# Mixing units in another order, weight blocks at other steps, one cast and one rest for a group's queries and keys, first load in one queue

## The chip, the cores and the metric

One core of a Trainium2 chip runs the whole program. The metric is the device time in microseconds (us). The kernel before takes 1590.1 us, the median of three runs.

## What is computed

```python
# q, k, v: (8, 12, 448, 64); w_ch1: (768, 3072); w_ch2: (3072, 768)
scores = q @ k.T / sqrt(64) - log(448)
attn   = 1 / (1 + exp(-scores))                  # a sigmoid, no row sums
x      = (attn @ v), heads joined                # (8, 448, 768)
mixed  = real(fft(fft(x, axis=1), axis=2))       # over tokens, then over channels
u      = x + mixed
un     = (u - mean(u)) / sqrt(var(u) + 1e-6)
out    = u + relu(un @ w_ch1) @ w_ch2
```

## The kernel before

The program has two stages. The first, some 410 us long, holds the attention, the Fourier mixing and the preparation of the weights, side by side; the second is the feed-forward network, whose 1180 us are nearly all matmuls. The change touches the first stage only.

**Steps.** The first stage is a written order. A loop counts steps `t` up to 204, two at a time; eight steps are one *group* `gg` (four heads of a batch: two sub-groups `w` of two heads, called `g = 2*gg + w`). There are 24 groups, three to each of the 8 batches. A group has four parts of two steps:

- part 0: `half_values` of the group before, `half_scores`, then the work entered for these steps, then `values` of the group before for `w = 0`
- part 1: two `scores`, the entered work, `values` for `w = 1`
- part 2: two `scores`, the entered work, and then `mix_some`, which takes mixing units worth 4.9 us by the kernel's own costs from the list
- part 3: two `scores`, the entered work

Work is entered with `at(step, ...)`: loads, casts, rests, folds, weight steps. `pin()` fixes on each engine the order in which the program was written. So an engine that waits holds up everything written behind it on that engine.

**Attention.** A load brings a group's queries and keys (tile `qk`). A *cast* copies them to a reduced format (`qh`, `kh`) on ScalarE, a *rest* forms what the copy lost (`ql`, `kl`) on VectorE. The scores (TensorE) go to two double PSUM banks `sc`, the sigmoid (ScalarE) brings them to SBUF as `a`. For the first two sub-groups the casts run on GpSimd and VectorE.

**Mixing.** A batch's mixing consists of 36 units. GpSimd first folds the attention result `xT` into `xp` (`FOLDS`). Then four `stage_d` outputs `d` of six units each (matmuls with the cosine and sine table `cd_sb` into `psd`, copied by ScalarE to `A`); four `stage_s` units `s` (one matmul from `A` into `pss`; of a pair, the first is copied by ScalarE to `Q`, the second is added to and subtracted from `Q` by VectorE, giving `sm` and `df`); and eight `add_x` units `x` (three transposes of `xT` into `psx`, to which VectorE adds `sm` or `df`, giving `u`). All of them, and the two `av` tiles of `values`, share four PSUM banks (pool `ps_m`). Batch `b` is mixed in the groups `3b+4`, `3b+5` and `3b+6`, below called its first, second and third mixing group. The last batch is mixed behind the attention, between pieces of the network's first matmuls (`mix_rest`, `fill`).

**Weights.** 48 blocks pass through five steps: a load (SyncE, tile `wr`, 4 buffers), an absolute value on ScalarE (`wt`; each block reuses the buffer of the block five before it), a maximum on VectorE, three bit operations on VectorE (0.56, 0.96 and 0.96 us), a store to `t_dram`. The list `ends` says at which step each block's bit operations stand, and the offsets beside it when the other steps do. Later, `pair` brings the stored blocks back and scales them.

Of the kernel before, what the change touches and what calls it, by code (L numbers as in the profile page):

```python
# [52 lines left out]
def spectral_attention_ffn(tc, qk, v, w1, w2, cd, cs, ident_in, out):  # L53
# [8 lines left out]
    with ExitStack() as top:  # L62
# [19 lines left out]
        if True:  # L82
# [7 lines left out]
            cd_sb = c1.tile([128, 2, 2, 3, 193], F32, name="cd_sb")  # L90
            cs_sb = c1.tile([128, 2, 2, HM], F32, name="cs_sb")

            raw, split, att, vrs, xts = {}, {}, {}, {}, {}

            def load_qk(gg, parts=1):
                b, r = divmod(gg, NG)
                t = io.tile([128, 2 * (SQ + S)], F32, tag="qk", name="qk")
                for w in range(2):
                    o = w * (SQ + S)
                    raw[2 * gg + w] = (t[:, o:o + SQ], t[:, o + SQ:o + SQ + S])  # L100
                step = 2 * (SQ + S) // parts
                for x in range(parts):
                    cols = slice(x * step, (x + 1) * step)
                    (nc.scalar if x else nc.sync).dma_start(t[:, cols], qk[b, r][:, cols])

            def load_v(gg):
                b, r = divmod(gg, NG)
                vrs[gg] = vr = io.tile([128, 896], F32, tag="vr", name="vr")
                nc.sync.dma_start(vr, v[b, r])

            def cast(g, n, e=None):
                split[g, n, 0] = t = wk.tile([128, (SQ, S)[n]], F32R, tag=("qh", "kh")[n], name=("qh", "kh")[n])
                if g > 1:
                    nc.scalar.activation(t, raw[g][n], AF.Copy)
                else:
                    (e or nc.gpsimd).tensor_scalar(
                        out=t, in0=raw[g][n], scalar1=1.0, scalar2=0.0, op0=ALU.mult, op1=ALU.add)

            def rest(g, n):
                split[g, n, 1] = t = wk.tile([128, (SQ, S)[n]], F32R, tag=("ql", "kl")[n], name=("ql", "kl")[n])  # L120
                nc.vector.tensor_tensor(
                    out=t, in0=raw[g][n], in1=split[g, n, 0].bitcast(F32), op=ALU.subtract)

            def sigmoid(ps):
                a = wk.tile([CP, 2, SQ], F32, tag="a", name="a", bufs=ABUF)
# [4 lines left out]
            def scores(gg, n):  # L130

                w, c = divmod(n, 3)
                g = 2 * gg + w
                ps = ps_sc.tile([128, 2, 512], F32, tag="sc", name="sc")
                for n, (kn, qn) in enumerate(((0, 0), (0, 1), (1, 0))):
                    for j in range(2):
                        h = slice(j * D, (j + 1) * D)
                        nc.tensor.matmul(  # L138
                            ps[:, j, :SQ], split[g, 1, kn][h, c * CP:(c + 1) * CP], split[g, 0, qn][h],
                            start=(n == 0), stop=(n == 2))  # L140
                att[g, c] = sigmoid(ps)

# [62 lines left out]
            def mix_units(b):  # L205
                xT, xp = xts[b]
                A = fx.tile([HM, 2, 2, 386], F32, tag="A", name="A")
                ps_d, sd, ut = {}, {}, {}

                def stage_d(kp, c, par, p):  # L210
                    m = HM - kp
                    if par == 0 and p == 0:
                        ps_d[c, kp] = ps_m.tile([128, 512], F32, tag="m", name="psd")
                    ps = ps_d[c, kp]
                    nc.tensor.matmul(
                        ps[:HM, par * 193:par * 193 + 193], xp[:, kp ^ c, c, par, p],
                        cd_sb[:, c, par, p], start=(p == 0), stop=(p == 2))
                    if par == 1 and p == 2:
                        act_next.append(lambda: nc.scalar.activation(
                            A[:, kp, c].rearrange("s (i r) -> s r i", r=2),  # L220
                            ps[:HM, 0:386].rearrange("s (r i) -> s r i", r=2), AF.Copy))

                def stage_s(kp, c):
                    m = HM - kp
                    ps = ps_m.tile([128, 512], F32, tag="m", name="pss")
                    nc.tensor.matmul(
                        ps[:m, :385], cs_sb[:HM, kp, c, :m], A[:, kp, c, :385], start=True, stop=True)
                    if c == 1:
                        sd["Q", kp] = Q = fx.tile([128, 385], F32, tag="Q", name="Q", bufs=2)
                        act_next.append(lambda: nc.scalar.activation(Q[:m], ps[:m, :385], AF.Copy))  # L230
                    else:
                        Q = sd["Q", kp]
                        sd[kp] = [fx.tile([128, 385], F32, tag=n, name=n) for n in ("sm", "df")]
                        for o, op in zip(sd[kp], (ALU.add, ALU.subtract)):
                            dve_next.append(lambda o=o, op=op: nc.vector.tensor_tensor(
                                out=o[:m], in0=ps[:m, :385], in1=Q[:m], op=op))

                def add_x(kp, r, hf):

                    lo, hi = (1, HM - 1) if r and not kp else (0, HM - kp)  # L240
                    s, d = sd[kp]
                    if hf == 0:
                        ut[kp, r] = fx.tile([128, DM], F32, tag="u", name="u", bufs=4)
                    u = ut[kp, r]
                    ps = ps_m.tile([128, 512], F32, tag="m", name="psx")
                    for i in range(3):
                        nc.tensor.transpose(
                            ps[:HM - kp, i * 128:(i + 1) * 128], xT[:, hf * 3 + i, r, kp:HS:2], ident)
                    y = d if hf == r else s
                    m = HM - kp  # L250
                    ysl = y[:m, 384:0:-1] if hf else y[:m, 0:384]

                    def add():
                        nc.vector.tensor_tensor(
                            out=u[:m, hf * 384:hf * 384 + 384], in0=ps[:m, :384], in1=ysl, op=ALU.add)
                        if hf:
                            base = b * S + (0, 113, 225, 336)[2 * r + kp] - lo

                            cut = lo + (hi - lo) // 16 * 16
                            for i, j in ((lo, cut), (cut, hi)):  # L260
                                if i < j:
                                    sp_next.append(lambda i=i, j=j: nc.sync.dma_start(
                                        u_dram[base + i:base + j, :], u[i:j, :]))
                    dve_next.append(add)


                def units_d(kp, c):
                    return [(0.33, lambda par=par, p=p: stage_d(kp, c, par, p)) for par in range(2) for p in range(3)]

                def units_s(kp, c):  # L270
                    return [(0.65, lambda: stage_s(kp, c))]

                def units_x(kp, r):
                    return [(ADD_US, lambda hf=hf: add_x(kp, r, hf)) for hf in range(2)]

                last = units_d(1, 0)
                res = (units_d(0, 1) + units_d(0, 0) + units_d(1, 1) + units_s(0, 1) + last[:3] + units_s(0, 0)
                       + last[3:] + units_x(0, 0) + units_s(1, 1) + units_x(0, 1) + units_s(1, 0)
                       + units_x(1, 0) + units_x(1, 1))
                return res  # L280

            wtile = {}
            worder = [(i, f) for f in range(NFC) for i in range(2)]
# [207 lines left out]
            load_qk(0, 2)  # L491
            load_v(0)
            for g in range(2):
                cast(g, 1)
                cast(g, 0, nc.gpsimd if g else nc.vector)
                rest(g, 0)
                rest(g, 1)
            load_qk(1)
            load_v(1)
            TQ = 4 * G  # L500
# [3 lines left out]
            def at(t, fn):  # L504
                extra.setdefault(t, []).append(fn)
# [6 lines left out]
            for gg in range(1, GG):  # L512
                if gg > 1:
                    at(8 * gg - 4, lambda n=gg: load_v(n))
                    at(max(8 * gg - 12, 6), lambda g=gg: load_qk(g))
                for w in range(2):
                    for n, fn in enumerate((cast, rest)):
                        at(8 * gg - 4 + 2 * n + 2 * w, lambda g=2 * gg + w, fn=fn: (fn(g, 0), fn(g, 1)))
            at(17, lambda: nc.sync.dma_start(cd_sb, cd))
            at(22, lambda: (nc.sync.dma_start(cs_sb, cs), nc.sync.dma_start(ident, ident_in)))  # L520
            ends = sorted([(t, (-10, -3, -1, 0, 3)) for t in range(19, TP, 8)]
                          + [(t, (-11, -5, -2, 0, 3)) for t in range(32, TP, 8)]
                          + [(t, (-10, -4, -2, 0, 3)) for t in (46, 54, 62, 70, 78, 86, 94, 158)])
            for n, (t, ds) in enumerate(ends[:2 * NFC]):
                for step, d in enumerate(ds):
                    at(t + d, lambda n=n, step=step: weight(n, step))
# [537 lines left out]
```

## Time and profile before

| | |
|---|---|
| median of three runs | 1590.1 us (1589.99 to 1591.21) |
| the profiled execution: time, span | 1589.42 us, 1587.6 us |
| TensorE matmul busy | 1559.5 us, 98% |
| VectorE busy | 1287.0 us, 81% |
| ScalarE busy | 657.9 us, 41% |
| GpSimd busy | 318.4 us, 20% |
| mean granted TensorE clock | 0.997 |

The time is the device's; the span reaches from the first instruction to the last, and 1.8 us lie around it. Shares are means over two unlike stages. For the first stage the busy time by group, the waits and the timeline say more than the page does.

### The profile page before, as it was taken

The numbers are of one execution on the slowest core, as the hardware profiler recorded it, in microseconds if no ns is written. First come the engines' busy times: TensorE is split into PE (matmuls) and PEld (weight loads), VectorE is DVE, ScalarE is ACT, GpSimd is POOL, SyncE is SP. The second block draws the span as 40 slices with busy tenths as digits, with TensorE's granted clock in tenths as the row PEclk, the third lists the DMA queues.
The fourth block names the chain that finished last, engine by engine and source line by source line (L and its number), as shares of the span: only waits on it lengthen the run. The fifth ranks groups of instructions, "written<-read, shape, count | busy, mean of one in ns | idle before, by whom it ended". The sixth has DMA issues, their size and how long they took to land.

```text
span 1587.6 us, 27518 instructions
## 1 busy us (share of the span) xinstructions
PE 1559.5 (98%) x11056; PEld 1064.9 (67%) x11056; DVE 1287.0 (81%) x2396; ACT 657.9 (41%) x823; POOL 318.4 (20%) x248
## 2 busy tenths in 40 slices
PE   8999999999999999999999999999999999999998
PEld 3555565555555557777777777777777777777775
DVE  4798899973798946887888888888788878887778
ACT  7876777774545434322232323222423232313221
POOL 3532444436888820000000000000000000000000
PEclk9999999999999999999999999999999999999999
DMA  6887978973788877568667766866776776576571
GB/s 244 299 295 284 347 262 291 335 246 107 249 280 295 323 304 304 186 262 277 236 199 304 231 235 235 295 204 267 259 254 181 282 298 232 166 296 255 200 270 50
DMA packets 130400, 402.43 MB, mean 253 GB/s; under 512 B 68833, under 2 KB 70113, under 8 KB 111713
## 3 DMA queue, kind: packets, MB, share of 16 engines
q1 hardware_dynamic: 130128, 400.22, 70.6%
q8 instruction: 86, 1.41, 0.4%
q10 hardware_dynamic: 144, 0.46, 0.1%
q14 instruction: 42, 0.34, 0.1%
HBM read 311.39 MB, written 73.92 MB: 243 GB/s over the span
## 4 chain that ended last, share of the span: by engine, by line
PE 66%; DVE 5%; DMA 2%; issue 1%; ACT 1%; SPq 0%; DVEq 0%; ACTq 0%
PE psf L815 29%; PE pso L871 29%; PE po L599 4%; PE psh L579 3%; DVE wp L439 1%; DMA ws<-w_dram 1%; DMA U<-u_dram 1%; DVE F L821 1%; DVE H L821 0%; ACT H L850 0%; DVE hl L587 0%; DVE ur L620 0%; DVE ur L899 0%; DVE acc L948 0%; DVE acc L886 0%
## 5 line engine op out<-in xcount | busy, mean ns | idle before, releaser
L815 PE MATMUL psf<-ut,ws 128*128 128x256 f16 x4536 | 506.7, 273 | 1.9 <-DVE ur L620 1.2
L871 PE MATMUL pso<-ws,H 128*128 128x384 f16 x3024 | 503.4, 326 | 1.0 <-DVE H L821 0.9
L815 PEld LDWEIGHTS <-ws 128*128 128x128 f16 x4536 | 443.4, 98 | 62.0 <-DMA ws<-w_dram 2.1
L871 PEld LDWEIGHTS <-H 128*128 128x128 f16 x3024 | 295.6, 98 | 189.9 <-DVE H L821 1.7
L840 ACT ACTIVATE F<-F 128x1024 f32<-128x1024 f32 x72 | 76.1, 1057 | 406.6 <-DVE F L821 406.6
L886 DVE TENSOR_TENSOR acc<-pso,acc 128x384 f32<-128x384 f32 x399 | 207.8, 550 | 19.9 <-PE pso L871 19.9
L821 DVE TENSOR_TENSOR H<-F,H 128x1024 f16<-128x1024 f32 (+1 forms) x144 | 155.3, 1087 | 48.8 <-ACT H L850 48.6
L126 ACT ACTIVATE a<-sc 128x900 f32<-128x900 f32 x168 | 147.5, 920 | 56.4 <-PE sc L138 50.7
L850 ACT ACTIVATE H<-F 128x1792 f16<-128x1792 f32 x72 | 122.2, 1697 | 111.0 <-DVE F L821 111.0
L821 DVE TENSOR_TENSOR F<-X,psf 128x256 f32<-128x256 f32 x288 | 117.1, 418 | 59.1 <-PE psf L815 55.1
L447 POOL TENSOR_TENSOR wq<-wq 128x384 f32<-128x384 f32 x96 | 150.5, 1573 | 32.5 <-DVE wp L439 26.9
L821 DVE TENSOR_TENSOR F<-F 128x256 f32<-128x256 f32 x288 | 109.5, 421 | 24.8 <-ACT F L840 20.1
L176 PE MATMUL av<-a,vr 128*64 128x450 f32 x576 | 119.1, 549 | 0.0
L439 DVE SCALAR_TENSOR_TENSOR wp<-wq,wsc,wp 128x1536 f16<-128x1536 f32 x48 | 99.4, 2104 | 21.8 <-ACT wp L437 21.8
L821 DVE TENSOR_TENSOR X<-X,psf 128x256 f32<-128x256 f32 x216 | 89.8, 416 | 18.6 <-PE psf L815 16.9
L579 PE MATMUL psh<-ut,wp 128*128 128x512 f16 x432 | 98.5, 379 | 0.0
L196 POOL TENSOR_TENSOR eo<-xT 128x450 f32<-128x450 f32 x48 | 53.4, 1132 | 205.1 <-ACT xT L184 198.1
L829 ACT ACTIVATE X<-psf 128x256 f32<-128x256 f32 x72 | 27.8, 386 | 155.5 <-PE psf L815 155.5
L599 PE MATMUL po<-wp,hh 128*128 128x256 f16 (+1 forms) x384 | 88.5, 326 | 0.0
L437 ACT ACTIVATE wp<-wq,wsc 128x1536 f16<-128x1536 f32 x48 | 73.5, 1570 | 25.0 <-DMA wq<-t_dram 20.7
L176 PEld LDWEIGHTS av<-a,vr 128*64 128x64 f32 x576 | 37.1, 136 | 69.6 <-issue 69.6
L579 PEld LDWEIGHTS <-wp 128*128 128x128 f16 x432 | 42.2, 98 | 49.1 <-issue 0.5
(87 smaller groups left out, 1623.6 us busy)
## 6 DMA issues: line engine op xcount, KB each, us to landing
ws<-w_dram SPq DMA_DIRECT2D x144, 1344.0 KB, 8.8
wr<-w_in SPq DMA_DIRECT2D x48, 768.0 KB, 7.8
w_dram<-wp SPq DMA_DIRECT2D x24, 1344.0 KB, 8.8
qk<-qk_in SPq DMA_DIRECT2D x23, 898.0 KB, 8.5
t_dram<-wt SPq DMA_DIRECT2D x48, 384.0 KB, 6.1
wq<-t_dram SPq DMA_DIRECT2D x24, 768.0 KB, 6.6
vr<-v_in SPq DMA_DIRECT2D x24, 448.0 KB, 5.1
U<-u_dram SPq DMA_DIRECT2D x24, 384.0 KB, 5.4
```

The costliest lines, as they stand in the source:

```text
L126: nc.scalar.activation(a, ps[:, :, :SQ], AF.Sigmoid, bias=-math.log(S), scale=1.0 / math.sqrt(D))
L176: nc.tensor.matmul(ps[j * D:(j + 1) * D, :SQ], vr[:, h:h + D], a[:, j], start=False, stop=(c == 2))
L439: nc.vector.scalar_tensor_tensor(out=w[:, 1, part], in0=t, scalar=sc, in1=w[:, 0, part], op0=ALU.mult, op1=ALU.subtract)
L447: nc.gpsimd.tensor_tensor(out=t[:, o], in0=t[:, x], in1=t[:, y], op=op)
L579: nc.tensor.matmul(hs[c, f], l[:, m], r[:, m], start=(m == n == 0), stop=(m == NCC - 1 and n == 2))
L599: nc.tensor.matmul(po[n][:, at:at + hi - lo], l[:, cols], r[:, lo:hi], start=(f == 0 and m == 0 and at == 0), stop=(f == NFC - 1 and m == ...
L815: nc.tensor.matmul(ps[:, :TH], w[:, x, a, m * 128:(m + 1) * 128], ut[y][:, b, m], start=(m == n == 0), stop=(m == n == 2))
L821: nc.vector.tensor_tensor(out=o, in0=x, in1=y, op=op)
L840: nc.scalar.activation(F[:, 0:4], F[:, 0:4], AF.Relu)
L850: nc.scalar.activation(hts[P][:, 0], F[:, 1:8], AF.Copy)
L871: nc.tensor.matmul(ps[:, :384], H[:, x, a, tp * 128:(tp + 1) * 128], w[:, y, b], start=(j == n == 0 and half != 1), stop=(j == 1 and n == ...
L886: later(0, lambda: nc.vector.tensor_tensor(out=to, in0=ps[:, :384], in1=to, op=ALU.add))
```

## The change

It has four parts.

1. The units of a batch's mixing stand in another order. With `d0 d1 d2 d3`, `s0` to `s3` and `x0` to `x7` in the order of their lists, they were `d0 d1 d2 s0 d3(1-3) s1 d3(4-6) x0 x1 s2 x2 x3 s3 x4 x5 x6 x7`. Now they are `d0 d1 s0 d2(1-2) s1 d2(3-5) x0 d2(6) x1 d3(1) x2 d3(2-6) s2 x3 s3 x4 x5 x6 x7`.
2. The weight blocks start at step 11 instead of 19 (and 24 instead of 32), and the extra ones, by which some groups hold three blocks instead of two, stand at steps 34, 58, 82, 154, 162, 178 instead of 46, 54, 62, 70, 78, 86, 94, 158. So the extra blocks of the first three batches fall into a first mixing group each.
3. Queries and keys of a sub-group are cast by one ScalarE instruction of 898 columns instead of two of 450 and 448, and their rest is one VectorE instruction. For the first two sub-groups ScalarE casts the keys and VectorE the queries; GpSimd casts nothing.
4. The two halves of the first load are both issued by SyncE; before, ScalarE issued the second.

```diff
-            def cast(g, n, e=None):
-                split[g, n, 0] = t = wk.tile([128, (SQ, S)[n]], F32R, tag=("qh", "kh")[n], name=("qh", "kh")[n])
+            def cast(g):
+                hi, lo = (wk.tile([128, SQ + S], F32R, tag=n, name=n) for n in ("hi", "lo"))
+                split[g] = [[x[:, :SQ] for x in (hi, lo)], [x[:, SQ:] for x in (hi, lo)], hi, lo]
                 if g > 1:
-                    nc.scalar.activation(t, raw[g][n], AF.Copy)
...
+                    nc.scalar.activation(hi, raws[g], AF.Copy)
+                    return
+                nc.scalar.activation(split[g][1][0], raw[g][1], AF.Copy)
+                nc.vector.tensor_scalar(
+                    out=split[g][0][0], in0=raw[g][0], scalar1=1.0, scalar2=0.0, op0=ALU.mult, op1=ALU.add)
+
+            def rest(g, n=slice(0, SQ + S)):
+                hi, lo = (x[:, n] for x in split[g][2:])
+                nc.vector.tensor_tensor(out=lo, in0=raws[g][:, n], in1=hi.bitcast(F32), op=ALU.subtract)
...
-                    (nc.scalar if x else nc.sync).dma_start(t[:, cols], qk[b, r][:, cols])
+                    nc.sync.dma_start(t[:, cols], qk[b, r][:, cols])
...
-                res = (units_d(0, 1) + units_d(0, 0) + units_d(1, 1) + units_s(0, 1) + last[:3] + units_s(0, 0)
...
+                return (d[0] + d[1] + s[0] + d[2][:2] + s[1] + d[2][2:5] + x[:1] + d[2][5:] + x[1:2] + d[3][:1]
+                        + x[2:3] + d[3][1:] + s[2] + x[3:4] + s[3] + x[4:])
...
-            ends = sorted([(t, (-10, -3, -1, 0, 3)) for t in range(19, TP, 8)]
...
+            ends = sorted([(t, (-10, -3, -1, 0, 3)) for t in range(11, TP, 8)]
+                          + [(t, (-11, -5, -2, 0, 3)) for t in range(24, TP, 8)]
+                          + [(t, (-10, -4, -2, 0, 3)) for t in (34, 58, 82, 154, 162, 178)])
```

What this moves is seen at three places. On TensorE, in the second mixing group of batch 0 (`psd` are the `d` units, `pss` the `s`, `psx` the `x`), before:

```order
L215 MATMUL psd<-cd_sb,xp 113x193 x3
L226 MATMUL pss<-A,cs_sb 113x385
L215 MATMUL psd<-cd_sb,xp 113x193 x3
L226 MATMUL pss<-A,cs_sb 113x385
L215 MATMUL psd<-cd_sb,xp 113x193 x3
L247 MATMUL psx<-ident,xT 113x128 x6
```

and in the changed kernel:

```order
L217 MATMUL psd<-cd_sb,xp 113x193
L228 MATMUL pss<-A,cs_sb 113x385
L217 MATMUL psd<-cd_sb,xp 113x193 x3
L249 MATMUL psx<-ident,xT 113x128 x3
L217 MATMUL psd<-cd_sb,xp 113x193
L249 MATMUL psx<-ident,xT 113x128 x3
L217 MATMUL psd<-cd_sb,xp 113x193
L249 MATMUL psx<-ident,xT 113x128 x3
L217 MATMUL psd<-cd_sb,xp 113x193 x3
```

The second `s` of the pair stands one unit behind the group's start instead of seven, and `x` and `d` units follow it; the seventh row, the first unit of `d3`, takes the bank that the second `s` held, and so stands behind `sm` and `df` on VectorE.

On TensorE, in the third mixing group, before:

```order
L226 MATMUL pss<-A,cs_sb 112x385
L247 MATMUL psx<-ident,xT 113x128 x6
L226 MATMUL pss<-A,cs_sb 112x385
L247 MATMUL psx<-ident,xT 112x128 x12
L138 MATMUL sc<-qh,kh 128x450 x2
```

and now:

```order
L217 MATMUL psd<-cd_sb,xp 113x193 x2
L228 MATMUL pss<-A,cs_sb 112x385
L249 MATMUL psx<-ident,xT 113x128 x3
L228 MATMUL pss<-A,cs_sb 112x385
L249 MATMUL psx<-ident,xT 112x128 x12
```

The last two units of `d3` have moved into this group, one `x` has left it, and the second `s` reads the `A` that ScalarE copies from the `d3` finished here.

On VectorE, in the second mixing group of batch 6, where `wp` is a scaled weight pair, before:

```order
L439 SCALAR_TENSOR_TENSOR wp_3840<-wq,wsc,wp_3840 128x1536
L235 TENSOR_TENSOR sm<-pss,Q 113x385
L235 TENSOR_TENSOR df<-pss,Q 113x385
L254 TENSOR_TENSOR u<-psx,df 113x384
L254 TENSOR_TENSOR u<-psx,sm 113x384
```

and now:

```order
L441 SCALAR_TENSOR_TENSOR wp_3654<-wq,wsc,wp_3654 128x1536
L237 TENSOR_TENSOR sm<-pss,Q 113x385
L237 TENSOR_TENSOR df<-pss,Q 113x385
L256 TENSOR_TENSOR u<-psx,df 113x384
L256 TENSOR_TENSOR u<-psx,sm 113x384 x2
```

The scaling of the weight pair stands ahead of `sm` as before, and a third addition `u` has come into the group.

More of the change, by code (lines that the diff above doesn't have):

```diff
@@ L91, in spectral_attention_ffn @@
             cs_sb = c1.tile([128, 2, 2, HM], F32, name="cs_sb")
-            raw, split, att, vrs, xts = {}, {}, {}, {}, {}
+            raw, raws, split, att, vrs, xts = {}, {}, {}, {}, {}, {}
             def load_qk(gg, parts=1):
@@ L100, in load_qk @@
                     raw[2 * gg + w] = (t[:, o:o + SQ], t[:, o + SQ:o + SQ + S])
+                    raws[2 * gg + w] = t[:, o:o + SQ + S]
                 step = 2 * (SQ + S) // parts
@@ L109, in load_v @@
                 nc.sync.dma_start(vr, v[b, r])
-            def cast(g, n, e=None):
-                split[g, n, 0] = t = wk.tile([128, (SQ, S)[n]], F32R, tag=("qh", "kh")[n], name=("qh", "kh")[n])
+            def cast(g):
+                hi, lo = (wk.tile([128, SQ + S], F32R, tag=n, name=n) for n in ("hi", "lo"))
+                split[g] = [[x[:, :SQ] for x in (hi, lo)], [x[:, SQ:] for x in (hi, lo)], hi, lo]
                 if g > 1:
[L114 to L122, printed above, removed]
+                    nc.scalar.activation(hi, raws[g], AF.Copy)
[6 more added lines that the diff above has]
+                nc.vector.tensor_tensor(out=lo, in0=raws[g][:, n], in1=hi.bitcast(F32), op=ALU.subtract)
             def sigmoid(ps):
@@ L138, in scores @@
                         nc.tensor.matmul(
-                            ps[:, j, :SQ], split[g, 1, kn][h, c * CP:(c + 1) * CP], split[g, 0, qn][h],
+                            ps[:, j, :SQ], split[g][1][kn][h, c * CP:(c + 1) * CP], split[g][0][qn][h],
                             start=(n == 0), stop=(n == 2))
@@ L274, in units_x @@
                     return [(ADD_US, lambda hf=hf: add_x(kp, r, hf)) for hf in range(2)]
-                last = units_d(1, 0)
-                res = (units_d(0, 1) + units_d(0, 0) + units_d(1, 1) + units_s(0, 1) + last[:3] + units_s(0, 0)
-                       + last[3:] + units_x(0, 0) + units_s(1, 1) + units_x(0, 1) + units_s(1, 0)
-                       + units_x(1, 0) + units_x(1, 1))
-                return res
+                d = [units_d(kp, c) for kp in range(2) for c in (1, 0)]
+                x = [u for kp in range(2) for r in range(2) for u in units_x(kp, r)]
+                s = [units_s(kp, c) for kp in range(2) for c in (1, 0)]
+                return (d[0] + d[1] + s[0] + d[2][:2] + s[1] + d[2][2:5] + x[:1] + d[2][5:] + x[1:2] + d[3][:1]
+                        + x[2:3] + d[3][1:] + s[2] + x[3:4] + s[3] + x[4:])
             wtile = {}
@@ L493, in spectral_attention_ffn @@
             for g in range(2):
[L494 to L497, printed above, removed]
+                cast(g)
+                rest(g, slice(0, SQ))
+                rest(g, slice(SQ, SQ + S))
             load_qk(1)
@@ L517, in spectral_attention_ffn @@
                     for n, fn in enumerate((cast, rest)):
-                        at(8 * gg - 4 + 2 * n + 2 * w, lambda g=2 * gg + w, fn=fn: (fn(g, 0), fn(g, 1)))
+                        at(8 * gg - 4 + 2 * n + 2 * w, lambda g=2 * gg + w, fn=fn: fn(g))
             at(17, lambda: nc.sync.dma_start(cd_sb, cd))
             at(22, lambda: (nc.sync.dma_start(cs_sb, cs), nc.sync.dma_start(ident, ident_in)))
-            ends = sorted([(t, (-10, -3, -1, 0, 3)) for t in range(19, TP, 8)]
-                          + [(t, (-11, -5, -2, 0, 3)) for t in range(32, TP, 8)]
-                          + [(t, (-10, -4, -2, 0, 3)) for t in (46, 54, 62, 70, 78, 86, 94, 158)])
+            ends = sorted([(t, (-10, -3, -1, 0, 3)) for t in range(11, TP, 8)]
+                          + [(t, (-11, -5, -2, 0, 3)) for t in range(24, TP, 8)]
+                          + [(t, (-10, -4, -2, 0, 3)) for t in (34, 58, 82, 154, 162, 178)])
             for n, (t, ds) in enumerate(ends[:2 * NFC]):
```

## The prediction

> **What bounds the kernel now.** I read the busy time by stage first. TensorE is busy nearly everywhere, so a gain must come from where it stands still or runs slowly; a view of the waits over the mixing groups says why it stands, and the busy time by group says where. In the rows below, one group each, the columns are the stretch in us, its length, and for each engine the busy time (and instructions), then TensorE's granted clock, the share of DMA and GB/s.
>
> ```profile
> 65.42:81.33 15.91, 15.91 (x108) 9.60 (x104) 11.25 (x19) 12.63 (x20) 6.03 (x7) 1.00 0.70 258
> 81.33:99.41 18.08, 16.63 (x103) 9.01 (x99) 16.65 (x29) 12.00 (x18) 5.93 (x6) 0.91 0.80 290
> 115.32:132.88 17.56, 16.45 (x109) 9.57 (x105) 13.03 (x21) 12.51 (x20) 6.92 (x7) 1.00 0.94 350
> 132.88:152.98 20.10, 18.08 (x102) 9.29 (x98) 18.75 (x32) 12.71 (x20) 5.95 (x7) 0.84 0.72 264
> 168.98:185.34 16.36, 16.18 (x108) 9.60 (x104) 12.41 (x21) 12.49 (x20) 5.90 (x6) 1.00 0.97 357
> 185.34:202.70 17.36, 14.91 (x102) 8.01 (x98) 17.01 (x27) 11.02 (x17) 7.70 (x7) 1.00 0.87 302
> 234.46:250.67 16.21, 14.88 (x102) 8.03 (x98) 15.93 (x25) 11.62 (x18) 7.94 (x7) 1.00 0.88 281
> 282.43:298.68 16.25, 14.89 (x102) 8.03 (x98) 15.97 (x25) 11.60 (x18) 8.03 (x7) 1.00 0.97 273
> 330.50:345.53 15.03, 14.57 (x103) 8.12 (x98) 12.34 (x22) 11.13 (x17) 6.08 (x6) 1.00 0.77 254
> ```
>
> These are the second and third mixing groups of batch 0, of batch 1 and of batch 2, then the third of 3, 4 and 5. A second group without a wait takes 15.91 us (first row); a third one needs 14.57 (TensorE's busy time in the last row) and takes up to 20.10. Two things are to be seen: where the third groups are long VectorE is full (16.65, 18.75, 17.01 us), and in two the clock was granted at 0.91 and 0.84. Over these groups VectorE is what TensorE waits for, and five times ScalarE stands behind a weight store:
>
> ```profile
> PE psx L247 <- DVE u L254: 6.3, 5, 2.4
> ACT wt L303 <- DMA t_dram<-wt: 10.7, 5, 3.2
> ```
>
> The clock falls behind such waits. In batch 0's third group three short ones (timeline of TensorE, the bracket is the wait and its releaser) precede two microseconds at half the clock (busy time by stretch again):
>
> ```profile
> 92.68 1.05 PE L247 MATMUL psx<-ident,xT 128*112 128x128 f32 x6 [0.55 <-DVE u L254]
> 94.16 0.59 PE L247 MATMUL psx<-ident,xT 128*112 128x128 f32 x3 [0.43 <-ACT Q L230]
> 95.22 0.90 PE L247 MATMUL psx<-ident,xT 128*112 128x128 f32 x3 [0.47 <-DVE df L235]
> ```
>
> ```profile
> 96.00:98.00 2.00, 2.00 (x11) 1.77 (x12) 2.00 (x5) 0.35 (x1) 1.34 (x2) 0.50 1.02 426
> ```
>
> **Weight blocks.** The same 48 blocks take the same loads, copies, bit operations and stores; only their steps move. Before, batches 0 to 2 had three blocks in each group, VectorE 3.4 us more each than with two. Now the third block lies in first mixing groups, where mixing asks nothing of VectorE. A `wt` buffer came free, by the list, 5 steps ahead of its next use at six blocks, and the five waits of 10.7 us are such places; now it is 8 or more until step 155, then once 5 (step 160) and once 6. The stores and loads stand earlier in SyncE's queue by as much as their blocks; the first load, now at step 1, goes ahead of the load for group 2, which isn't needed for 12 steps. So the old waits of batches 0 to 2 should go: third groups 18.08 + 20.10 + 17.36 - 3 x 14.57 = 11.83, second groups 17.56 + 16.36 - 2 x 15.91 = 2.10, together 13.9 us.
>
> **The new order, third mixing group.** It brings a wait of its own. The second `s` reads the `A` of the `d3` finished two units before, which ScalarE copies behind two sigmoids and the cast. What stands there in batch 3:
>
> ```profile
> 242.57 1.73 ACT L126 ACTIVATE a<-sc 128x900 f32<-128x900 f32 x2 [0.32 <-PE sc L138]
> ...
> 243.01 0.90 PE L226 MATMUL pss<-A,cs_sb 113*112 113x385 f32 x2
> ...
> 243.75 0.82 PE L247 MATMUL psx<-ident,xT 128*113 128x128 f32 x6
> ...
> 244.18 0.58 ACT L114 ACTIVATE qh<-qk 128x450 fp32r<-128x450 f32 x1
> ...
> 244.40 0.81 PE L226 MATMUL pss<-A,cs_sb 113*112 113x385 f32 x2
> ...
> 244.65 0.58 ACT L114 ACTIVATE kh<-qk 128x448 fp32r<-128x448 f32 x1
> ...
> 245.12 0.49 ACT L230 ACTIVATE Q<-pss 112x385 f32<-112x385 f32 x1
> ...
> 246.52 0.37 PE L247 MATMUL psx<-ident,xT 128*112 128x128 f32 x1 [1.31 <-DVE u L254]
> ```
>
> Mixing starts at 243.01, ScalarE is free of the casts at 245.12, 2.11 later. An `x` takes 0.33 (two between 243.75 and 244.40), an `s` 0.65, a `d` 0.33 (rows of batch 3 below). TensorE is done with two `d`, `s` and `x` at 0.66 + 0.65 + 0.33 = 1.64; `A` is there at 2.02 + 0.53 = 2.55 (0.09 for the shorter cast), so `s` waits 0.9. The last `x` takes its bank, behind `sm` and `df`: `s` ends at 3.25, 0.2 until VectorE starts and 1.0 for both give 4.45, TensorE is there at 4.2: 0.25 more. I take 1.2 us in each of six batches. Batches 0 to 2: 3.6 instead of 13.9, -10.3. Batches 3 to 5 lose 16.21 + 16.25 + 15.03 - 3 x 14.57 = 3.8 today: 3.6 instead, -0.2. The `d` units that the third group gains and the `x` it loses (0.3) the second gives back.
>
> **The new order, second mixing group.** The first unit of `d3` is there at 0.36 + 0.65 + 0.99 + 0.33 x 3 = 3.0 us after mixing starts, and waits for `df`. Before, nothing of TensorE waited for VectorE here. In batches 0 to 2 VectorE is free in time. In batches 3 and 4 it carries the normalization, and is late:
>
> ```profile
> 208.72 0.96 DVE L317 SCALAR_TENSOR_TENSOR wt<-wr,wt 128x768 int32<-128x768 int32 x1
> ...
> 227.13 1.24 PE L215 MATMUL psd<-cd_sb,xp 128*113 128x193 f32 x6
> 227.28 1.34 DVE L312 TENSOR_SCALAR wt<-wt 128x768 int32<-128x768 int32 x1
> ...
> 228.21 0.81 PE L226 MATMUL pss<-A,cs_sb 113*113 113x385 f32 x2
> ...
> 228.86 1.15 PE L215 MATMUL psd<-cd_sb,xp 128*113 128x193 f32 x6
> ...
> 229.85 0.81 PE L226 MATMUL pss<-A,cs_sb 113*113 113x385 f32 x2
> ...
> 230.31 1.62 DVE L317 SCALAR_TENSOR_TENSOR wt<-wr,wt 128x768 int32<-128x768 int32 x1
> ...
> 231.85 0.55 DVE L235 TENSOR_TENSOR sm<-pss,Q 113x385 f32<-113x385 f32 x1
> ...
> 232.32 0.55 DVE L235 TENSOR_TENSOR df<-pss,Q 113x385 f32<-113x385 f32 x1
> ```
>
> `df` is done at 232.87, 5.74 after the start of mixing at 227.13: a wait of 2.75 as it stands. But the three bit operations run beside GpSimd's folds and take 1.34 + 1.62 + 1.62, where the second and third take 0.96 without it (first row) and the first 0.56. Four joined rests ahead of them, each 0.07 us shorter by my estimate (0.62 us for 450 columns and 0.95 for 768 leave 0.15 for an instruction's start, about half of it hidden by the one before), and what they spare beside an earlier fold put VectorE about a microsecond ahead, and then most of the first operation runs before the fold starts: I take 1.8 us, which leaves a wait of 1.0, and 0.2 for the addition that the next `x` waits for. Bounds: 0 and 2.9; taken 1.2, twice: +2.4. Batch 5 has one third block more than today, 3.4 us of VectorE in two groups; VectorE's idle time there takes it up, since the normalization is over by then (12.34 busy of 15.03 in its third group); 0, at worst 1.
>
> Batch 6 has the scaling of a weight pair ahead of `sm`:
>
> ```profile
> 370.02 1.24 PE L215 MATMUL psd<-cd_sb,xp 128*113 128x193 f32 x6
> ...
> 372.80 2.05 DVE L439 SCALAR_TENSOR_TENSOR wp<-wq,wsc,wp 128x1536 f16<-128x1536 f32 x1 [7.36 <-ACT wp L437]
> ...
> 374.77 0.55 DVE L235 TENSOR_TENSOR sm<-pss,Q 113x385 f32<-113x385 f32 x1
> ...
> 375.24 0.55 DVE L235 TENSOR_TENSOR df<-pss,Q 113x385 f32<-113x385 f32 x1
> ```
>
> `df` at 375.79 is 5.77 behind the start: TensorE waits 2.8, and hands over 2.5 later than today. A wait of that length should bring the slow clock. What that costs is read from batch 1's third group: 18.08 busy at a mean clock of 0.84, against 14.57: 3.5; batch 0's is 16.63 - 14.57 = 2.1. I take 1.7, which is half of a slow stretch of 3.4 us. Behind it TensorE waits for GpSimd today, which finishes its folds at its own time:
>
> ```profile
> 391.39 0.42 PE L215 MATMUL psd<-cd_sb,xp 128*113 128x193 f32 x1 [1.40 <-POOL xp L202]
> ```
>
> That 1.4 (and 0.2 elsewhere) is given back: 2.5 + 1.7 - 1.6 = +2.6.
>
> The Trainium skill, TensorE: Matmul & The Clock Gate, Part 1, counts activity in windows of about 3.4 us and warns of idle gaps longer than that. By this rule no wait here, the longest 2.9, would slow the clock, and batch 6 would cost 0.9 instead of 2.6. The rows of batch 0 disagree: 1.45 us of waits in three pieces slowed it. I go by the rows.
>
> **Joined casts and rests, the first load.** A cast of 898 columns by two of 0.58, whose starts lie 0.47 apart, saves about 0.09 of ScalarE, which counts only in the four groups without mixing: two casts in each make 0.7, of which I take -0.2, as little of it is waited for. On VectorE nothing waits for rests beyond what stands above. At the start ScalarE copies keys before its first sigmoid and so loads two tables instead of one:
>
> ```profile
> 1.14 1.28 ACT L126 ACT_TABLE_LOAD   x1 [1.14 <-PEq L1051]
> ...
> 5.25 0.40 DVE L116 TENSOR_SCALAR qh<-qk 128x450 fp32r<-128x450 f32 x1 [5.25 <-DMA qk<-qk_in]
> ...
> 7.12 0.92 ACT L126 ACTIVATE a<-sc 128x900 f32<-128x900 f32 x1 [4.70 <-PE sc L151]
> ```
>
> Two key copies from 5.25 (0.47 and 0.58) and a table of 1.28 end at 7.6, where the first sigmoid starts at 7.12 today. The second half of the load is issued some 0.4 us later, but the first then has the engines alone. Between 0 and 0.9: +0.4. The last batch, between the network's first matmuls, has the same new dependences with more work between them: between 0 and 1.5, +0.4.
>
> **The sum.** -10.3 - 0.2 + 2.4 + 2.6 - 0.2 + 0.4 + 0.4 = -4.9 us: the profiled execution's 1589.42 to 1584.5, and from the median of 1590.1, 0.7 above it, to 1585.2, 0.3% less. A measurement of this kernel tells 0.2%, 3.2 us, from no change.
>
> **Rivals.**
>
> *VectorE doesn't get ahead in batches 3 and 4.* If it keeps its place against TensorE, both wait 2.9 instead of 1.2, and such a wait brings the slow clock there too: 2 x (1.7 + 1.7) = 6.8, 1592.0, no difference. For it: VectorE is busy without a gap there, so 1.8 us must come from GpSimd's overlap alone. Chance 0.27.
>
> *The new wait of the third groups slows the clock.* It is 1.2 us in six groups; 1.45 sufficed in batch 0, while one wait of 2.4 in batch 2 (17.36 us at clock 1.00) did not, so where the waits fall decides. At 1.7 each, six give 10.2: 1595.4, slower; five of them suffice for slower. Against it: 1.31 in batch 3 and as much in batch 4 went without. Chance 0.16.
>
> *All the waits on VectorE vanish.* If it is a little further ahead, batches 3 and 4 lose nothing, and if batch 6's wait keeps the clock, 2.4 + 1.7 more is gained: 1581.1. Chance 0.2.
>
> My forecast has 0.37. Faster by over 0.2% (below 1586.9) are the last rival and four fifths of the forecast: 0.5. Within 0.2%: the first rival and the rest of the forecast, 0.34. Slower: 0.16. The range reaches from the last rival, less 1.1 for a start and a tail without loss, to just under the slow one: 1580.0 to 1594.5; beyond it lie most of the second rival's chance and little below. The forecast's own range is 1583 to 1588.
>
> **What the profile will show.** Right: third groups of batches 0 to 2 between 15.5 and 16.2 us at clock 1.00; no wait of ScalarE for a store before 300 us; in each third group a wait of some 0.9 of `pss` for `A`; in batch 6's second group one of 2.8 of `psd` for `df`, and the wait for GpSimd near 391 us gone. Waits of `psd` for `df` above 2 us in batches 3 and 4 would speak for the first rival, a clock under 1.00 in third groups for the second. Wrong altogether would be third groups of batches 0 to 2 as long as before: then the third block wasn't their cause.

## The result, and the profile after

The changed kernel is slower by 0.6%: 1598.88 us median (six runs, 1596.52 to 1602.63) against 1590.03 (1587.89 to 1591.21), ratio 1.0061, interval [1.0043, 1.0079]. The forecast was 1585.2, 0.3% faster. The six runs lie in two sets of three, 1596.5 to 1596.9 and 1600.9 to 1602.6. The profiled execution is the slowest of them, 1602.63 us (span 1600.8), against 1589.42 (1587.6) before.

What TensorE waits for in the first 420 us (engine, line, what is waited for: us in total, times, longest):

```profile
PE psd L217 <- DVE df L237: 9.6, 4, 3.1
PE pss L228 <- ACT A L221: 5.7, 8, 1.3
...
PE psx L249 <- DVE df L237: 3.7, 8, 2.3
```

The first two are new, the third was 1.3 us before. Busy time by group, columns as in the prediction: second and third groups of batches 0, 1 and 2, then of 3, 4 and 5:

```profile
65.28:83.25 17.97, 16.09 (x109) 9.47 (x105) 16.87 (x22) 10.95 (x15) 8.74 (x7) 1.00 0.88 319
83.25:99.26 16.01, 15.10 (x104) 8.43 (x99) 11.12 (x17) 11.22 (x16) 6.29 (x6) 1.00 0.75 272
...
115.17:130.76 15.59, 15.59 (x109) 9.45 (x105) 12.31 (x19) 10.96 (x15) 7.89 (x7) 1.00 0.76 272
130.76:146.76 16.00, 15.10 (x104) 8.42 (x99) 11.14 (x17) 11.23 (x16) 6.29 (x6) 1.00 0.83 304
...
162.68:178.26 15.58, 15.58 (x109) 9.45 (x105) 12.30 (x19) 10.97 (x15) 7.87 (x7) 1.00 0.75 265
178.26:194.27 16.01, 15.11 (x103) 8.41 (x99) 11.14 (x17) 11.23 (x16) 6.27 (x6) 1.00 0.87 309
...
210.18:230.20 20.02, 17.60 (x109) 10.40 (x105) 17.52 (x23) 11.86 (x16) 8.10 (x6) 0.91 0.72 233
230.20:246.22 16.02, 15.11 (x104) 8.43 (x100) 12.65 (x18) 11.65 (x17) 6.65 (x6) 1.00 0.66 214
...
262.12:282.28 20.16, 17.69 (x109) 10.74 (x105) 17.43 (x23) 11.56 (x16) 8.13 (x6) 0.92 0.73 239
282.28:298.28 16.00, 15.11 (x104) 8.43 (x100) 12.65 (x18) 11.81 (x17) 6.88 (x6) 1.00 0.82 260
...
314.19:335.95 21.76, 18.68 (x110) 11.54 (x105) 17.31 (x24) 12.04 (x16) 8.52 (x7) 0.84 0.89 328
335.95:351.94 15.99, 15.10 (x103) 8.44 (x99) 11.13 (x17) 11.08 (x16) 6.05 (x6) 1.00 0.64 221
```

The third groups of batches 0 to 2, 18.08, 20.10 and 17.36 us before, all take 16.0 now: that part of the forecast came. Most of the loss is in the second groups of batches 3, 4 and 5: 20.02, 20.16 and 21.76 us, where before they took:

```profile
218.59:234.46 15.87, 15.87 (x108) 9.61 (x104) 15.64 (x22) 12.56 (x20) 7.86 (x6) 1.00 0.65 191
...
266.56:282.43 15.87, 15.87 (x108) 9.61 (x104) 15.60 (x22) 12.55 (x20) 7.85 (x6) 1.00 0.85 233
...
314.59:330.50 15.91, 15.91 (x108) 9.60 (x104) 12.95 (x21) 11.91 (x19) 6.64 (x6) 1.00 0.83 295
```

(The rest is lost in batch 0's second group, 17.97 us, and from batch 6's second group on.) In batch 3 VectorE works without a gap up to `df`, and the timeline shows how TensorE comes to stand behind it:

```profile
218.67 1.34 DVE L314 TENSOR_SCALAR wt<-wt 128x768 int32<-128x768 int32 x1
218.76 0.58 PE L217 MATMUL psd<-cd_sb,xp 128*113 128x193 f32 x2
...
220.05 1.62 DVE L317 SCALAR_TENSOR_TENSOR wt<-wr,wt 128x768 int32<-128x768 int32 x1
...
221.70 1.62 DVE L319 SCALAR_TENSOR_TENSOR wt<-wr,wt 128x768 int32<-128x768 int32 x1
...
223.24 0.55 DVE L237 TENSOR_TENSOR sm<-pss,Q 113x385 f32<-113x385 f32 x1
...
223.71 0.54 DVE L237 TENSOR_TENSOR df<-pss,Q 113x385 f32<-113x385 f32 x1
...
224.31 0.58 PE L217 MATMUL psd<-cd_sb,xp 128*113 128x193 f32 x2 [2.35 <-DVE df L237]
```

Mixing starts at 218.76 and reaches the first unit of `d3` 3.20 us later; `df` ends at 224.25, 5.49 after the start, and TensorE stands 2.35 us. Behind such waits the clock halves (busy time in four stretches; the clock is the third number from the right):

```profile
226.00:229.41 3.41, 3.41 (x18) 2.22 (x16) 2.14 (x4) 0.92 (x1) 0.32 (x1) 0.50 0.95 308
277.19:280.60 3.41, 3.41 (x15) 2.82 (x16) 2.60 (x5) 0.00 (x0) 1.11 (x2) 0.50 0.97 295
328.39:335.22 6.83, 6.18 (x27) 4.76 (x31) 4.04 (x8) 0.92 (x1) 1.60 (x2) 0.50 0.92 342
383.01:386.42 3.41, 3.41 (x15) 2.83 (x16) 1.26 (x3) 0.00 (x0) 3.41 (x4) 0.50 0.34 104
```

Together 17.1 us at half speed, up to 8.5 us lost.

### The profile page after: what moved, and what is told of

Read it like the earlier page. It is cut to its first block, busy times and chain, and to the rows that moved or that the text cites. A ratio compares the mean times of both kernels' runs of the same rounds, so it can differ in the third digit from the quotient of the medians.

```text
span 1600.8 us, 27412 instructions
## 1 busy us (share of the span) xinstructions
PE 1564.5 (98%) x11056; PEld 1068.4 (67%) x11056; DVE 1282.2 (80%) x2351; ACT 656.2 (41%) x780; POOL 324.8 (20%) x245
## 4 chain that ended last, share of the span: by engine, by line
PE 66%; DVE 4%; DMA 1%; ACT 1%; issue 1%; POOL 1%; SPq 0%; DVEq 0%; ACTq 0%; POOLq 0%
PE psf L816 29%; PE pso L872 29%; PE po L600 4%; PE psh L580 3%; DVE wp L441 1%; DVE F L822 1%; DMA U<-u_dram 1%; DMA ws<-w_dram 1%; POOL wq L449 1%; DVE H L822 0%; ACT H L851 0%; DVE ur L621 0%; DVE ur L900 0%; DVE acc L949 0%; DVE acc L887 0%
## 5 line engine op out<-in xcount | busy, mean ns | idle before, releaser
L124 DVE TENSOR_TENSOR lo<-qk,hi 128x898 fp32r<-128x898 f32 (+2 forms) x50 | 57.3, 1149 | 41.2 <-ACT hi L116 41.1
L217 PE MATMUL psd<-cd_sb,xp 128*113 128x193 f32 x384 | 79.8, 344 | 9.9 <-DVE df L237 9.6
```

Source lines behind the costliest of these rows:

```text
L217: nc.tensor.matmul(ps[:HM, par * 193:par * 193 + 193], xp[:, kp ^ c, c, par, p], cd_sb[:, c, par, p], start=(p == 0), stop=(p == 2))
```

## Experiments

The theory: the new order of units costs all that is lost and more, because the first unit of `d3` in the second mixing group stands behind `df`; the weight steps alone would have been a gain. The rivals: weight blocks at late steps; the start; the joined casts and rests. Five kernels split the change into its parts (each ratio is taken against runs of the kernel before on the same chip; their medians lay between 1589.1 and 1590.0):

| kernel | order | weight steps | casts, start | median us | ratio to before, interval |
|---|---|---|---|---|---|
| before | old | old | old | 1590.03 | 1 |
| e4_casts_start_only | old | old | new | 1587.96 | 0.9997 [0.9988, 1.0006] |
| e3_steps_only | old | new | old | 1577.91 | 0.9927 [0.9914, 0.9939] |
| e1_old_order | old | new | new | 1577.75 | 0.9924 [0.9912, 0.9937] |
| e2_order_only | new | old | old | 1601.56 | 1.0081 [1.0067, 1.0095] |
| e9_order_steps | new | new | old | 1600.06 | 1.0065 [1.0052, 1.0078] |
| changed kernel | new | new | new | 1598.88 | 1.0061 [1.0043, 1.0079] |

**The old order in the changed kernel.**

```diff
-                return (d[0] + d[1] + s[0] + d[2][:2] + s[1] + d[2][2:5] + x[:1] + d[2][5:] + x[1:2] + d[3][:1]
-                        + x[2:3] + d[3][1:] + s[2] + x[3:4] + s[3] + x[4:])
+                last = units_d(1, 0)
+                res = (units_d(0, 1) + units_d(0, 0) + units_d(1, 1) + units_s(0, 1) + last[:3] + units_s(0, 0)
...
```

> The changed kernel with its mixing units in the old order; weight steps, joined casts and start stay. Theory 1 (the new order behind sm and df costs all that is lost, some 15 to 20 us from batch 3 on, and the weight steps give the 8 to 14 that batches 0 to 2 gained): 1577 to 1582 us, no wait of psd for df, clock 1.00 in batches 3 to 6. Theory 2 (the weight blocks at steps 154, 162 and 178 make VectorE late in batches 5 and 6 whatever the order): 1585 to 1590, with waits of psx for df or u and a low clock left in batches 5 and 6. Theory 3 (start and joined casts cost several us): as theory 1, but group 1 starts over 1 us later than in the kernel before and the time is 1582 to 1585.

1577.75 us: the theory's number, 21 below the changed kernel. The second groups of batches 3 and 5 (busy time by group):

```profile
205.19:221.10 15.91, 15.91 (x109) 9.60 (x104) 15.32 (x20) 12.37 (x18) 7.87 (x6) 1.00 0.66 208
...
300.87:316.78 15.91, 15.91 (x109) 9.60 (x104) 14.87 (x21) 12.44 (x18) 8.48 (x7) 1.00 0.92 335
```

In batch 3 VectorE is about as busy as in the kernel before (15.32 of 15.91 us), and TensorE waits for nothing in these groups. The late weight blocks are there too, and cost batch 5 nothing in this order.

**The new order alone, the weight steps alone, casts and start alone.** In the kernel before, each by the lines that the diff above shows.

> The kernel before with nothing but the new order of units. Theory 1: the four waits of psd for df in the second mixing groups of batches 3 to 6 (2.3 to 3.1 us each in the changed kernel) and the slow clock behind them (1.7 to 3.4 each) are here too, so 1600 to 1606 us. Theory 2: batch 5 has no block at 162 here, so its second group has no wait over 1 us, and the time is 1592 to 1597. If order and weight steps only go wrong together: 1588 to 1591.

1601.56 us, as the theory says, though not by the places it named: only batches 4 and 6 have the wait for `df`. Here the third groups of batches 0 to 2 keep their third weight block and are as long as before or longer, as in batch 2:

```profile
184.66:205.42 20.76, 17.41 (x104) 10.07 (x99) 20.21 (x29) 11.72 (x18) 10.58 (x8) 0.84 0.90 331
```

Behind such a group VectorE has caught up with TensorE: in batch 3's second group, which starts at 221.33, `df` ends 11.4 us behind the start (14.1 in the changed kernel), and the group takes 15.86 us. Two of the three bit operations ahead of it start before GpSimd's fold does (229.22), and take 0.55 and 0.96 us instead of 1.34 and 1.62:

```profile
228.61 0.55 DVE L312 TENSOR_SCALAR wt<-wt 128x768 int32<-128x768 int32 x1
229.20 0.96 DVE L315 SCALAR_TENSOR_TENSOR wt<-wr,wt 128x768 int32<-128x768 int32 x1
230.20 1.62 DVE L317 SCALAR_TENSOR_TENSOR wt<-wr,wt 128x768 int32<-128x768 int32 x1
...
232.21 0.54 DVE L235 TENSOR_TENSOR df<-pss,Q 113x385 f32<-113x385 f32 x1
```

Where the weight steps take the delay of the third groups away, it comes back in the second ones: they are worth 11.5 us in the old order and 1.5, less than the runs can tell, in the new one (1601.56 - 1600.06).

> The kernel before with nothing but the new weight steps. Theory 1: third mixing groups of batches 0 to 2 fall from 18.1, 20.1 and 17.4 us to 14.6 to 16, no wait of ScalarE for a weight store in batches 0 to 2, 1576 to 1581 us. Theory 2: the same there, but batches 5 and 6 give back 5 or more: 1582 to 1590. If the third block was not the cause of the long groups: 1589 to 1592.

1577.91 us, third groups of batches 0 to 2 at 15.0 us: the third block was their cause. Batch 5 gives nothing back; from batch 6's second group to the end 2.1 us more go by than before, with a longer wait for GpSimd's fold.

> The kernel before with the joined casts and rests and the new start, old order, old weight steps. By the prediction's terms (start +0.4, casts -0.2): 1589.5 to 1591. Theory 3 (the start costs 1.2 us, group 0 lasts 10.3 instead of 9.1): 1591 to 1592.5. Theory 4 (the rest waits for the whole joined cast, VectorE falls later behind GpSimd's folds, and third groups grow): above 1593.

No difference that can be told (0.9997). Group 1 starts at 14.49 us, in the kernel before at 14.36. These rivals fall.

> The kernel before with the new order of units and the new weight steps, casts, rests and start as before. Theory 1 (order and weight steps make the whole difference): as the changed kernel, 1596 to 1602 us, waits of psd for df in batches 0 and 3 to 5. Theory 4 (the rest that waits for a joined cast puts VectorE later, so the joined form shares in the loss): 1588 to 1594 us, with shorter waits for df.

Without the joined casts and rests the waits for `df` are no shorter (2.54, 2.59 and 3.21 us in batches 3 to 5), and the time is the same within the intervals.

**Another place for `d3`.** In the changed kernel:

```diff
-                return (d[0] + d[1] + s[0] + d[2][:2] + s[1] + d[2][2:5] + x[:1] + d[2][5:] + x[1:2] + d[3][:1]
-                        + x[2:3] + d[3][1:] + s[2] + x[3:4] + s[3] + x[4:])
+                return d[0] + d[1] + s[0] + d[2] + s[1] + x[:2] + d[3] + x[2:3] + s[2] + x[3:4] + s[3] + x[4:]
```

> The changed kernel with another order of units: d2 is finished ahead of the second s, so that the first unit of d3 takes the bank of d2 (freed by ScalarE's copy) and not that of the second s (freed by sm and df on VectorE). Theory 1a (the place of d3 in that bank is what loses the time): no wait of psd for df, second groups of batches 0 and 3 to 5 take 15.6 to 16 us at clock 1.00, the 0.7 us waits of pss for A stay, 1580 to 1585 us. Rival 1b (VectorE is late in any such order, and the next to take a bank behind df waits as long): a wait of 2 to 3 us at psx or av in the same groups, 1592 to 1600.

1581.96 us, 0.9954 [0.9941, 0.9966]. No `psd` waits for VectorE, and the second groups of batches 3 and 5 are:

```profile
207.70:223.31 15.61, 15.61 (x109) 9.50 (x105) 15.38 (x20) 11.49 (x16) 7.57 (x6) 1.00 0.67 203
...
304.59:320.24 15.65, 15.65 (x106) 9.48 (x101) 14.62 (x20) 11.58 (x16) 8.37 (x7) 1.00 0.92 341
```

So it isn't the new order as such: it is the first unit of `d3` in the bank that `df` frees, with six units between it and the `s` that `df` reads. Here it stands closer, with two units between, in a bank that ScalarE frees, and doesn't wait. Most of what is left above the old order (4 us) is in the third groups, which take 16.0 us in batches 0 to 2 and 16.7 to 16.9 in batches 3 to 5; in batches 3 and 4 a `pss` waits 1.6 us for `u`, which was not expected.

**Why `df` is late.** Two kernels take VectorE's work ahead of `df` away: one moves a block's bit operations behind the mixing, the other leaves one of them out.

```diff
-            ends = sorted([(t, (-10, -3, -1, 0, 3)) for t in range(11, TP, 8)]
+            ends = sorted([(t, (-10, -3, -1, 3, 6)) for t in range(11, TP, 8)]
```

> The changed kernel with the three bit operations (and the store) of one of the two weight blocks of each group three steps later, behind the mixing instead of ahead of sm and df on VectorE. Theory 1c (these operations, slowed beside GpSimd's folds, are what makes df late): the waits of psd for df in batches 0, 3, 4 and 5 are gone or under 0.5 us, batch 6's stays (a scaled weight pair stands there), 1582 to 1588 us. Rival (VectorE has 97% of its time taken in batches 3 and 4, so what is moved behind sm and df makes something else late): waits of psx for u or of psd for xp of 1 to 2 us each, 1590 to 1597.

1592.6 us, 1.0021 [1.0012, 1.003]: the rival's time, but not the waits that it named. Batches 0 and 5 have no wait for `df` left (batch 0's first group waits 1.39 us for `A` instead), batches 3 and 4 still wait 2.29 us; the second groups of batches 3 and 5:

```profile
209.18:229.20 20.02, 17.67 (x109) 10.67 (x105) 19.51 (x28) 11.79 (x16) 8.04 (x6) 0.91 0.65 194
...
313.04:328.85 15.81, 15.81 (x109) 9.40 (x105) 15.28 (x22) 11.44 (x16) 8.50 (x8) 1.00 1.01 389
```

In batch 3 the operations that left the second group's front were replaced by those which the first group pushed out. VectorE is busy 15.3 of 15.9 us in the first group too, so a shift gives `df` nothing there. Less work should; this kernel leaves a part of the computation out, to see what it costs:

```diff
-                    nc.vector.scalar_tensor_tensor(
-                        out=ti, in0=hi, scalar=-0x40000000, in1=ti, op0=ALU.bitwise_and, op1=ALU.bitwise_or)
+                    if ends[n][0] not in (104, 107, 112, 115, 128, 131, 136, 139):
+                        nc.vector.scalar_tensor_tensor(
+                            out=ti, in0=hi, scalar=-0x40000000, in1=ti, op0=ALU.bitwise_and, op1=ALU.bitwise_or)
```

> The changed kernel without the last of the three bit operations (the one that puts the sign back) in the eight weight blocks of the first and second mixing groups of batches 3 and 4; this part of the computation is left out. Theory 1d (VectorE has no idle time between the first group and df there, so df comes earlier by as much as is taken off ahead of it, 4 to 5 us with the folds' slowing): both waits of 2.4 us and the slow clock behind them go, the two second groups fall from 20.1 to 15.6 to 16 us, batch 5 stays, 1589 to 1592 us. Rival (df waits for Q or the matmuls ahead of it, not for VectorE's volume): 1597 to 1601.

1590.12 us, 8.8 below the changed kernel, as the theory says: the waits of batches 3 and 4 are gone. Batch 3's second group, and batch 5's, whose work is untouched:

```profile
208.51:224.11 15.60, 15.60 (x110) 9.45 (x106) 12.32 (x18) 11.62 (x16) 5.93 (x6) 1.00 0.78 208
...
303.46:324.10 20.64, 17.57 (x109) 10.60 (x105) 17.33 (x24) 11.67 (x16) 8.53 (x7) 0.92 0.91 335
```

**Batch 5's block.**

```diff
-                          + [(t, (-10, -4, -2, 0, 3)) for t in (34, 58, 82, 154, 162, 178)])
+                          + [(t, (-10, -4, -2, 0, 3)) for t in (16, 34, 58, 82, 154, 178)])
```

> The changed kernel with the extra weight block of step 162 (second group of batch 5) at step 16 instead. Theory 2, cut to this place: batch 5's second group falls from 21.8 us at clock 0.84 to 15.6 to 17, all else stays, 1591 to 1594 us. If the block there is not the cause: 1596 to 1600 and the group stays over 20 us.

1595.35 us, 1.0041 [1.0028, 1.0054]. Batch 5's second group falls to 15.60 us: the third block was its cause. The time is 1.4 above what was expected. In the profiled execution, the slowest of five, group 1 took 12.43 us (11.62 in the changed kernel) and batch 0's second group 19.78 (17.97), with a wait of 1.97 for `df` and a stretch of half clock behind it.

**The clock.** TensorE is kept busy where it would wait:

```diff
-                    for i in range(3):
+                    for i in [0, 1, 2] * (7 if 3 <= b <= 6 and (kp, r, hf) == (0, 0, 1) else 1):
```

> The changed kernel in which TensorE repeats the transposes of the second x seven times in batches 3 to 6 (18 more matmuls of 128 columns, some 2 us, just ahead of the unit that waits for df; the result is the same). Clock theory (some 8.5 of the 20 us lost are the half clock behind the waits): with TensorE busy the clock stays at 1.00 in batches 3 to 6, 1588 to 1593 us. If the clock falls for another reason than idle TensorE: 1597 to 1601. If the added matmuls only lengthen the groups: above 1601.

1593.64 us, 1.0029 [1.0018, 1.0039]: with more matmuls, 5.2 us less (0.6 above the expected range). Second groups of batches 3 and 5, and the added matmuls with the wait behind them in batch 3:

```profile
208.55:227.07 18.52, 18.05 (x128) 11.43 (x124) 17.52 (x23) 11.61 (x16) 8.12 (x6) 1.00 0.73 218
...
309.42:328.69 19.27, 18.09 (x128) 11.47 (x123) 17.31 (x24) 11.67 (x16) 8.51 (x7) 1.00 0.93 339
```

```profile
219.82 2.46 PE L249 MATMUL psx<-ident,xT 128*113 128x128 f32 x21
222.68 0.58 PE L217 MATMUL psd<-cd_sb,xp 128*113 128x193 f32 x2 [0.40 <-DVE df L237]
```

`d3` starts no earlier after the group's start, but the clock stays at 1.00, and the groups are 1.5 and 2.5 us shorter. Against the changed kernel's profiled execution the profiled one here gains 9.0; the median gains less, since other executions lose less to the clock. The granted clock over the whole execution bears this out: 0.998 to 1.000 in the eight runs of this kernel, 0.993 to 0.996 in the six of the changed one.

**Batch 6.**

```diff
-                for step, e in enumerate((0, 8 + p, 9 + p)):
+                for step, e in enumerate((0, 10, 11)):
```

> The changed kernel with the two scaled weight pairs two steps later, the first behind the last mixing units of batch 6's second group and no longer ahead of sm. By the prediction's term for batch 6 (a wait of 2.3 to 2.8, 1.7 of clock, 1.6 given back): the wait of psx for df near 383 us goes and 2.5 to 4.5 us come back, 1593 to 1596.5. If the pair is only late elsewhere (the network's first matmuls wait for it): 1597 to 1602, with a wait of psh for wp.

1594.08 us, 1.0026 [1.0016, 1.0035]; the wait near 383 us is gone, as expected. This run shows something else. Its second groups of batches 3 and 4, and in each the wait:

```profile
208.94:227.47 18.53, 16.09 (x110) 9.46 (x105) 17.53 (x23) 11.57 (x16) 8.12 (x6) 1.00 0.73 218
...
259.35:279.17 19.82, 17.45 (x110) 10.73 (x105) 17.41 (x23) 11.57 (x16) 8.12 (x6) 0.91 0.83 243
```

```profile
223.08 0.58 PE L217 MATMUL psd<-cd_sb,xp 128*113 128x193 f32 x2 [2.37 <-DVE df L237]
...
273.50 0.99 PE L217 MATMUL psd<-cd_sb,xp 128*113 128x193 f32 x2 [2.37 <-DVE df L237]
```

The same wait of 2.37 us kept the clock once and halved it once.

**A version faster than both.** The changed kernel with the old order and two blocks moved:

```diff
-                          + [(t, (-11, -5, -2, 0, 3)) for t in range(24, TP, 8)]
-                          + [(t, (-10, -4, -2, 0, 3)) for t in (34, 58, 82, 154, 162, 178)])
+                          + [(t, (-11, -5, -2, 0, 3)) for t in range(24, TP, 8) if t not in (120, 144)]
+                          + [(t, (-10, -4, -2, 0, 3)) for t in (34, 58, 70, 82, 94, 154, 162, 178)])
```

> A version meant to be faster than both: the changed kernel with the old order, and the weight blocks of steps 120 and 144 (third groups of batches 3 and 4, where TensorE still waits 1.06 us for u) at steps 70 and 94, behind the mixing of the second groups of batches 1 and 2. If VectorE's load there is all that is left of the waits: 1574.5 to 1577 us, third groups of batches 3 and 4 at 14.95 instead of 16.0 us. If the blocks at 70 and 94 crowd the buffers as the third blocks did in the kernel before: 1578 to 1582, with waits in batches 1 and 2.

1574.3 us, 0.9907 [0.9894, 0.9919]. Batch 1's third group, just behind one of the added blocks, takes 15.15 us (14.94 with the old order alone), and batch 3's, which lost its block, 14.95 instead of 16.01:

```profile
128.03:143.18 15.15, 14.91 (x103) 8.02 (x99) 14.80 (x23) 10.79 (x15) 7.12 (x6) 1.00 0.89 300
...
221.97:236.92 14.95, 14.60 (x102) 8.10 (x98) 11.35 (x17) 11.39 (x16) 6.18 (x7) 1.00 1.06 351
```

Its interval overlaps that of the old order without this move ([0.9912, 0.9937]), so the last 3 us are likely, not certain.

## Why the prediction was wrong, step by step

The profiled executions differ by 13.2 us in span (the medians by 8.9; the profiled one is the slowest of six); the groups' lengths above and in the prediction give where:

| term | predicted | measured |
|---|---|---|
| second and third groups of batches 0 to 2 | -10.3 | -8.2 |
| third groups of batches 3 to 5 | -0.2 | +0.5 |
| second groups of batches 3 and 4 | +2.4 | +8.4 |
| second group of batch 5 | 0 | +5.9 |
| from batch 6's second group to the end | +3.0 | +6.8 |
| the rest (start, casts) | +0.2 | -0.2 |
| sum | -4.9 | +13.2 |

- *Batches 0 to 2.* Right in its mechanism: without batch 0's second group the sum is 105.37 - 15.91 - (97.16 - 17.97) = 10.27 us less, the forecast's 10.3. But "in batches 0 to 2 VectorE is free in time" failed in batch 0, +2.06. VectorE is busy 16.87 us in that group (12.31 in batch 1's, which has the same blocks). It comes late out of the first group, whose last bit operation ends 2.0 us into the second (67.30 us; in batch 1 it ends 2.0 us ahead of it, at 113.12), so that the last block's bit operations run beside the fold, from 73.54 on, and take 1.02, 1.62 and 1.62 us; in batch 1 they run ahead of it, from 120.99 on, and take 0.56, 0.96 and 0.96. With the bit operations moved (e6_bits_late) this wait is gone, in the other runs with both parts it is 0.6 to 2.0 us. Why VectorE is later in batch 0's first group was not tried.
- *The new wait in third groups*: `pss` waits 0.70 for `A` and `psx` 0.20 for `df` in each of the six, forecast 0.9 and 0.25. That each third group takes 16.0 us comes from this and from the units that moved into it: TensorE is busy 15.1 us there, 14.57 before. With two casts instead of one (e9_order_steps) the wait for `A` is 0.79: the joined cast spares the 0.09 that was worked out for it.
- *"I take 1.8 us" of VectorE's lead in batches 3 and 4* is the step that failed first. `df` ends 5.49 us behind the start of mixing, 5.74 before: VectorE got 0.25 ahead. The bit operations still take 1.34, 1.62 and 1.62 us, still wholly beside GpSimd's folds. So the wait is 2.35 and 2.39 us where 1.0 was forecast, and the forecast has no half clock there; with it each group cost 4.2. The first rival was right on this (its wait of 2.9 is 0.5 too long); its total of 1592.0 left batches 0 and 5 and the end as forecast.
- *"VectorE's idle time there takes it up"* in batch 5 failed outright. The argument was made with its third group's load (12.34 of 15.03 us). The wait lies in the second, where three blocks stand ahead of `df`: 17.31 us busy, a wait of 3.08, twice 3.4 us of half clock. Without the third block the group takes 15.60 (e7_block_moved). A deadline in the middle of a group isn't met by idle time behind it.
- *Batch 6*: forecast a wait of 2.8, less 1.6 given back. It is 2.25 (with 0.28 ahead of it), at an `x` and not at the first unit of `d3` as the forecast said, with 3.41 us of half clock behind it. The 1.4 from GpSimd was indeed given back, but a wait of 1.50 for `xT` came in its place, and the last batch lost 1.28 where 0.4 was taken. Where these two come from was not tried:

```profile
382.75 0.78 PE L249 MATMUL psx<-ident,xT 128*113 128x128 f32 x3 [2.25 <-DVE df L237]
...
395.93 0.59 PE L249 MATMUL psx<-ident,xT 128*113 128x128 f32 x3 [1.50 <-ACT xT L186]
...
412.00 0.90 PE L228 MATMUL pss<-A,cs_sb 113*113 113x385 f32 x2 [1.28 <-ACT A L221]
```

- *The start* cost nothing, which the bounds 0 to 0.9 allowed.
- *The range* ended at 1594.5 because the slow clock was counted in third groups only (the second rival) or in batches 3 and 4 only (the first), never both waits and clock in four second groups at once.

One fault is behind most of it: the forecast asked how far VectorE is behind in each group by itself, and took off what would put VectorE ahead. Where an engine is busy 15.3 of 15.9 us, as in batches 3 and 4, it doesn't get ahead, and time that another change gives TensorE only makes it arrive earlier and wait longer.

## What to carry to other kernels

Ask of every unit that is moved which buffer it takes and which engine frees that buffer; if that engine is nearly full, the move turns its hidden lateness into a wait. Moving work about within that engine doesn't help where it is full in group after group, as in batches 3 and 4; less work, or a bank that another engine frees, did. A gain elsewhere on the waiting engine doesn't add up with such a move: here 11.5 us of gain shrank to 1.5. Count a wait of TensorE with the half clock behind it, as one of several outcomes.

## What the runs showed of the hardware

The half clock comes in stretches of exactly 3.41 us or twice that, on a fixed grid: in the changed kernel their starts lie 51.19, 51.20 and 54.62 us apart, which is 15, 15 and 16 times 3.413. The place of the grid differs from run to run. Laid over the waits of all the traces here, between 45 and 420 us, it gives a rule for this kernel: each of the 14 grid windows in which TensorE waited over 2.0 us in all was followed by one at half clock; no half clock began behind one with less than 1.40; between 1.40 and 2.0 both occurred. (Twice a half clock, once begun, went on for a second window although TensorE had waited only 0.65 and 0.16 us in the first.) So the place of a wait on the grid matters: in the run with the late weight pair the wait of 2.37 us in batch 4 lies with 2.26 us in one window and halved the clock, while that in batch 3 is cut by the grid into 1.48 and 0.89 and didn't; the two groups took 19.82 and 18.53 us. That single executions of the changed kernel spread over 6 us fits this, but was not tested by itself.

The Trainium skill, TensorE: Matmul & The Clock Gate, Part 1, gives a free-running window of 3413 ns, and the traces agree with both: stretches of 3.41 us, on a grid whose place differs from run to run. The rule that the Trainium skill draws there is to avoid idle gaps above about 3.4 us. The traces differ from that: waits of 2.25 to 2.39 us halved the clock here. Filling such waits with matmuls was worth 5.2 us.
